# Ranking the elementwise work between two matrix products above the decoding of weights in a hand-planned attention + two-FFN kernel

## The chip, the cores and the metric

One core of one Trainium2 chip runs the whole program. The metric is the device time of one launch in microseconds; the median of three runs is compared, and one further run was profiled.

## What is computed

All numbers are float32. Attention with RMS-normalised queries and keys feeds a squared-ReLU feed-forward layer ("layer 1"), and that feeds a gated one ("layer 2"):

```python
q_n, k_n = rmsnorm(q, g_q), rmsnorm(k, g_k)               # 4 batches, 12 heads, 448 rows, 64 wide
x = softmax(q_n @ k_n.T / 8) @ v                          # -> 1792 tokens x 768
h = x @ w_in;  r = maximum(h, 0.0)                        # d_ff 2048
x = (r * r) @ w_out                                       # layer 1
g = x @ w_gate;  val = x @ w_val                          # d_ff 1536
out = (g * (1.0 / (1.0 + exp(-g))) * val) @ w_out         # layer 2
```

## The kernel before

**Three matmuls for one product.** Each float32 operand of the feed-forward layers is kept as a pair of tiles, hi and lo, whose sum is the number. A product of two 128-row blocks is three matmuls, hi with hi, hi with lo and lo with hi (`mm3`, issued at L321). One block of d_ff (128 columns, called f) against the six blocks of d_model is 18 matmuls; `in_product` makes such a group, `h`, and `out_of` adds one f to the six output tiles `y`, again 18 matmuls.

**Decoding.** The weights arrive as 64-bit words and are decoded on the chip by `load_weights`. Each of its tiles (a key such as ("in", 7)) comes as two chunks of 384 columns. A chunk is a DMA on SP's queue (`raw`), one scaling on ScalarE (L272, `wa`), four instructions on VectorE (L282, L285, L288, L291), the sum (L295, VectorE or GpSimd), the cast to hi (L212) and the difference lo (L308, VectorE or GpSimd). Slots for decoded tiles are reused: 12 from the attention phase, 8 more after it.

**The elementwise work between the two products.** In layer 1 it is `squares` for every f: ReLU on ScalarE (L356, `r`), its square on ScalarE (L357, `s` hi), the exact square on VectorE (L358, which frees the PSUM bank of `h`), and the difference (L362, `s` lo). In layer 2 it is `gated` (L373 on ScalarE, L374 on VectorE) and `valued` (L384 on VectorE, L212 on ScalarE, L387 on VectorE). There are two PSUM banks for `h` (`h_free`), three tiles for `s`, and two for `r`.

**Sweeps.** `products` runs the feed-forward layers as a list of sweeps, each one batch against a range of f. The first sweep is the last batch with f = 0 to 9, whose first three `h` are made by `lead` while attention still runs; the second is batch 2 with f = 0 to 9. `products` is one generator, so the order of the matmuls is fixed: h of f, then `out_of` for f - 2 (BEHIND = 2), then h of f + 1, and so on. The inputs of the next sweep are loaded and split by `load_x` (DMA, L212 on ScalarE, L1113 on VectorE), six tiles one after another, while the present sweep runs.

**The planner.** All of this is put in order when the program is built. `simulate` plays the kernel through with a planned cost for each operation; whenever an engine comes free it takes, among what is ready, the operation whose thread has the lowest rank, and issues it there:

```python
job = min(q, key=lambda job: (job[0].rank, job[2]))
```

What comes out is a fixed order of instructions in each engine's queue. The ranks that stand around the change: `k` is the step of a sweep that a product belongs to (POST = 10000 plus one for each f of layer 1 and two for each f of layer 2). `squares`, `gated`, `valued` and `load_x` are spawned with rank k, the writing of finished sums (`written`) with k - 2, and a weight tile that is first needed at step `when` has

```python
items += [(key, None, when[key] - W_AHEAD) for key in later]
```

with W_AHEAD = 6, and its chunk c adds c / 10. So elementwise work of step k stands behind the decoding of every tile that is due before step k + 6.

Of the kernel before, what the change touches and what calls it, by code (L numbers as in the profile page):

```python
# [52 lines left out]
W_AHEAD = 6  # L53
# [19 lines left out]
def attention_two_ffn_kernel(  # L73
# [22 lines left out]
    def as_f32(ap):  # L96
        return ap.bitcast(F32)
# [42 lines left out]
    def spawn(gen, rank, is_local=False):  # L140
        t = Thread(gen, rank, is_local)
        local[0] += is_local
        resume(t, None)
        return t

    def resume(t, value):
        while True:
            try:
                p = t.gen.send(value)
            except StopIteration:  # L150
                local[0] -= t.is_local
                return
            value = None
            serial[0] += 1
            if callable(p):
                if p():
                    continue
                blocked.append((t, p))
            elif isinstance(p, tuple):
                job = [t, p, serial[0], False]  # L160
                for e in p[0]:
                    queues["V" if e == "W" else e].append(job)
            else:
                heapq.heappush(timers, (clock[0] + p, serial[0], t, None))
            return
# [162 lines left out]
    def in_product(ps, w, x):  # L328
        for kk in range(KD):
            yield from mm3(ps, w[0], w[1], bass.ts(kk, 128), x[kk][:, 0, :], x[kk][:, 1, :], kk == 0, kk == KD - 1)  # L330
# [6 lines left out]
    def tile_at(where, shape, dtype, name):  # L337
        return where[0].tile(shape, dtype, tag=where[1], name=name)

    def h_tile(name):  # L340
        yield lambda: h_free
        where = h_free.pop(0)
        return tile_at(where, [128, S], F32, name), where

    def squares(ps, where, n, s=None):

        yield settle["P"]
        s_at = None
        if s is None:
            yield lambda: s_free  # L350
            s_at = s_free.pop(0)
            s = tile_at(s_at, [128, 2, S], F32R, f"s_{n}")
        yield lambda: ea_free
        r_at = ea_free.pop(0)
        r = tile_at(r_at, [128, S], F32, f"r_{n}")
        yield {"A": 424}, lambda e: e.activation(out=r, in_=ps, func=ACTF.Relu)  # L356
        yield {"A": 467}, lambda e: e.activation(out=s[:, 0, :], in_=r, func=ACTF.Square)  # L357
        yield {"V": 535}, lambda e: e.scalar_tensor_tensor(  # L358
            out=r, in0=ps, scalar=0.0, in1=r, op0=ALU.max, op1=ALU.mult
        )  # L360
        (h_free if where[0] is ps_f else s_banks).append(where)
        yield {"W": 535, "G": 1106}, lambda e: e.tensor_tensor(  # L362
            out=s[:, 1, :], in0=r, in1=as_f32(s[:, 0, :]), op=ALU.subtract
        )
        ea_free.append(r_at)
        ready[n] = s, s_at
# [347 lines left out]
    def all_scores(me):  # L714
        for n in range(NT):
# [9 lines left out]
            def products(e):  # L725
# [6 lines left out]
                for p, (h, rows) in enumerate(parts):  # L732
                    for c in range(2):
# [3 lines left out]
                        )  # L737

            yield {"P": 760 if full else 406 * len(parts)}, products, 0
            scored[0] = n + 1  # L740
            for h, _ in parts:
# [128 lines left out]
    def all_values(me):  # L870


        for g in range(NH // 2):
            me[0].rank = PT * g + PT - 1 + T_LAG
            slabs = range(PT * g, PT * g + PT)
            yield lambda: all(n in turned_p for n in slabs) and g in vs and o_banks
            ps = [turned_p.pop(n) for n in slabs]
            vz, vz_at = vs.pop(g)
            o_at = o_banks.pop(0)
            o = tile_at(o_at, [128, S], F32, f"o{g}")  # L880
            steps = [(h, j) for j in (3, 0, 1, 2) for h, j in ((0, j), (1, j + 4 * (j < 3)))]

            def products(e):
                for i, (h, j) in enumerate(steps):
                    half = slice(64 * h, 64 * h + 64)
                    e.matmul(o[half], lhsT=vz[:, j, half], rhs=ps[j][0], start=(i < 2), stop=(i >= 6))  # L886

            yield {"P": 3500}, products, 0
            p_free.extend(at for _, at in ps)
            v_free.append(vz_at)  # L890
            spawn(outputs(g, o, o_at), PT * g + PT - 1 + T_LAG, True)
# [206 lines left out]
    def x_tiles(n, second, ts):  # L1098
        def tile_of(j):
            pool = xp2 if second and j < 4 else xp  # L1100
            ts.append(pool.tile([128, 2, S], F32R, tag=f"x{j + 2 if second and j >= 4 else j}", name=f"x_{n}_{j}"))
            return ts[j]

        return tile_of

    def load_x(src, n, tiles, done):

        def part(j, where):
            raw = tile_at(where, [128, S], F32, f"xr_{n}_{j}")
            yield from dma(lambda e: e.dma_start(out=raw, in_=src[j]), 128 * S * 4)  # L1110
            t = tiles(j)
            yield {"A": 467, "W": 300}, lambda e: copy(e, t[:, 0, :], raw)
            yield {"W": 535, "G": 1106}, lambda e: e.tensor_tensor(  # L1113
                out=t[:, 1, :], in0=raw, in1=as_f32(t[:, 0, :]), op=ALU.subtract
            )
            io_free.append(where)
            done.append(j)

        for j in range(KD):
            yield lambda: io_free  # L1120
            yield from part(j, io_free.pop(0))

    def release(key):
        del wt[key]
        free.append(placed.pop(key))
# [3 lines left out]
    def products():  # L1129
        behind = []  # L1130
        ys = {}
        xs = x1[LAST]
        k = POST
        for i, (layer, b, fs, last_use, partial, dst) in enumerate(sweeps):
            n = f"{layer}_{i}"
            done = None
            for f in fs:
                if f == fs[X_AT if len(fs) > 6 else 1] and i + 1 < len(sweeps):
                    nxt, done = [], []
                    src = (x1_d if sweeps[i + 1][0] == 1 else x2_d)[sweeps[i + 1][1]]  # L1140
                    spawn(load_x(src, n, x_tiles(n, i % 2 == 0, nxt), done), k)
                name = f"{n}_{f}"
                if i == 0 and f < 3:
                    pass
                elif layer == 1:
                    yield lambda: ("in", f) in wt
                    ps, where = yield from h_tile(f"h_{name}")
                    yield from in_product(ps, wt["in", f], xs)
                    spawn(squares(ps, where, name), k)
                    if f in last_use:  # L1150
                        release(("in", f))
                else:
                    sig = {"n": name}
                    for w, then in (("g", gated), ("v", valued)):
                        yield lambda: (w, f) in wt
                        ps, where = yield from h_tile(f"h_{w}_{name}")
                        yield from in_product(ps, wt[w, f], xs)
                        spawn(then(ps, where, sig), k)
                        if f in last_use:
                            release((w, f))  # L1160
                while len(behind) >= BEHIND:
                    yield from behind.pop(0)
                sums = Partial(partial, n) if partial and f == fs[-1] else None
                behind.append(out_of(name, n, layer, f, f == fs[0], f == fs[-1], f in last_use, ys, sums, dst, k))
                k += layer
            if done is not None:
                yield lambda: len(done) == KD
            xs = nxt
        for gen in behind:
            yield from gen  # L1170
        finished.append(0)
# [31 lines left out]
    def out_of(name, n, layer, f, first, last, release_it, ys, sums, dst, k):  # L1203
        key = ("out" if layer == 1 else "o2", f)
        yield lambda: key in wt and name in ready
        w = wt[key]
        s, where = ready.pop(name)
        for j in range(KD):
            if first:
                ys[j] = ps_y.tile([128, S], F32, tag=f"y{j}", name=f"y_{n}_{j}")  # L1210
            yield from mm3(ys[j], w[0], w[1], bass.ts(j, 128), s[:, 0, :], s[:, 1, :], first, last)
            if last:
                spawn(written(ys[j], sums, j, n, dst[j]), k - 2)
        s_free.append(where)
        if release_it:
            release(key)

    spawn(products(), 0)
    simulate(lambda: finished and not timers and not any(queues.values()))

# [80 lines left out]
```

## Time and profile before

| | us |
|---|---|
| median of three runs | 1360.04 |
| lowest, highest | 1357.88, 1381.38 |
| the profiled execution | 1357.86 |
| its span, first to last instruction | 1356.1 |
| TensorE busy in the span | 1298.6 |
| VectorE busy | 807.2 |
| ScalarE busy | 588.3 |

Attention with the first inner products lies from 0 to about 440 us, layer 1 from there to about 819 us, and layer 2 from there to the end. Busy time is the time in which an engine had an instruction in execution; what ended an idle time is inferred from semaphores. The mean granted clock of TensorE over the span was 0.982 of full speed.

### The profile page before, as it was taken

What the parts mean: (1) busy time and instruction counts of PE and PEld (TensorE: products, weight loads), DVE (VectorE), ACT (ScalarE), POOL (GpSimd) and SP (SyncE); (2) the same over time, 40 slices, a digit from 0 to 9 for tenths busy, and PEclk for the clock granted to TensorE, in tenths of its full rate; (3) what the DMA queues carried; (4) which work ended last, traced back from release to release, by engine and by line L of the source; (5) the groups of instructions that cost most, each with busy time, mean ns of one, the idle gap of its engine ahead of it and who ended that gap; (6) DMA issues with size and microseconds to landing.
All of it is one profiled execution on the core that took longest, in us unless ns stands there. A gap on an engine that the chain in (4) does not pass through costs nothing.

```text
span 1356.1 us, 18618 instructions
## 1 busy us (share of the span) xinstructions
PE 1298.6 (96%) x6522; PEld 1111.6 (82%) x6522; DVE 807.2 (60%) x1863; ACT 588.3 (43%) x1338; POOL 185.3 (14%) x178
## 2 busy tenths in 40 slices
PE   8788899999999889999999999999999999999998
PEld 5444576666778779999999999999999999999998
DVE  7899997866641957967932299622218971213122
ACT  5787888777762524443422244321204431201100
POOL 3444434543330000000000010000000000000000
PEclk8888999999999989999999999999999999999999
DMA  6676666666511424464540356320104530303021
GB/s 198 202 227 203 202 211 215 206 207 192 177 45 67 145 94 123 146 199 127 164 149 29 109 168 210 120 82 1 61 1 141 162 102 1 109 0 116 1 82 42
DMA packets 86241, 170.75 MB, mean 126 GB/s; under 512 B 12857, under 2 KB 59778, under 8 KB 86146
## 3 DMA queue, kind: packets, MB, share of 16 engines
q1 hardware_dynamic: 86146, 169.56, 39.6%
q8 instruction: 51, 0.84, 0.3%
q14 instruction: 44, 0.36, 0.1%
HBM read 141.82 MB, written 27.69 MB: 125 GB/s over the span
## 4 chain that ended last, share of the span: by engine, by line
PE 81%; DVE 8%; DMA 6%; ACT 2%; issue 1%; POOL 1%; SPq 0%; DVEq 0%; ACTq 0%; POOLq 0%
PE y L321 26%; PE h_v L321 13%; PE h_g L321 13%; PE h L321 13%; PE o L886 4%; PE sc L734 3%; PE ya L321 2%; PE h_a L321 2%; DMA rkb<-rkd 2%; PE pt L833 2%; DMA zb<-zd 1%; DVE sc L756 1%; ACT ring L765 1%; PE pt L831 1%; POOL kst L653 1%
## 5 line engine op out<-in xcount | busy, mean ns | idle before, releaser
L321 PE MATMUL y<-s,hi_out 128*128 128x448 f32 x624 | 178.6, 367 | 4.9 <-DVE s L362 4.9
L321 PE MATMUL h<-x,hi_in 128*128 128x448 f32 x588 | 169.1, 369 | 7.5 <-DVE r L358 7.5
L321 PE MATMUL h_v<-x,hi_v 128*128 128x448 f32 x576 | 163.5, 365 | 0.0
L321 PE MATMUL h_g<-x,hi_g 128*128 128x448 f32 x576 | 163.5, 365 | 0.0
L321 PE MATMUL y<-s,hi_o 128*128 128x448 f32 x576 | 163.5, 365 | 0.0
L374 DVE TENSOR_TENSOR sig<-h_g,sig 128x448 f32<-128x448 f32 x48 | 29.9, 623 | 191.3 <-ACT sig L373 191.3
L765 ACT ACTIVATE ring<-sc,m,rms 128x448 f32<-128x448 f32 x168 | 121.8, 726 | 32.2 <-DVE m L759 22.4
L756 DVE TENSOR_REDUCE sc<-sc 128x1 f32<-128x448 f32 x168 | 101.8, 625 | 48.1 <-PE sc L734 43.5
L321 PEld LDWEIGHTS y<-s,hi_out 128*128 128x128 f32 x624 | 118.1, 189 | 14.7 <-DVE s L362 5.3
L321 PEld LDWEIGHTS h<-x,hi_in 128*128 128x128 f32 x588 | 111.8, 190 | 17.1 <-DVE r L358 8.2
L734 PE MATMUL sc<-kst,qst 128*128 128x448 f32 x368 | 108.3, 400 | 16.2 <-ACT ring L765 12.8
L321 PEld LDWEIGHTS h_g<-x,hi_g 128*128 128x128 f32 x576 | 108.2, 188 | 8.5
L321 PEld LDWEIGHTS y<-s,hi_o 128*128 128x128 f32 x576 | 108.2, 188 | 8.5
L321 PEld LDWEIGHTS h_v<-x,hi_v 128*128 128x128 f32 x576 | 108.2, 188 | 8.5
L321 PE MATMUL y<-s,lo_out 128*128 128x448 f32 x312 | 114.6, 367 | 0.0
L373 ACT ACTIVATE sig<-h_g 128x448 f32<-128x448 f32 x48 | 26.0, 542 | 191.4 <-PE h_g L321 191.4
L321 PE MATMUL h<-x,lo_in 128*128 128x448 f32 x294 | 108.4, 369 | 0.0
L321 PE MATMUL h_g<-x,lo_g 128*128 128x448 f32 x288 | 105.2, 365 | 0.0
L321 PE MATMUL y<-s,lo_o 128*128 128x448 f32 x288 | 105.2, 365 | 0.0
L321 PE MATMUL h_v<-x,lo_v 128*128 128x448 f32 x288 | 105.2, 365 | 0.0
L212 ACT COPY p<-pt 128x448 f32<-128x448 f32 x166 | 86.3, 531 | 27.7 <-PE pt L833 19.7
L734 PEld LDWEIGHTS sc<-kst,qst 128*128 128x128 f32 x368 | 62.2, 193 | 29.9 <-ACT ring L765 17.1
(160 smaller groups left out, 2335.6 us busy)
## 6 DMA issues: line engine op xcount, KB each, us to landing
kq<-in_kq_t_dram SPq DMA_DIRECT2D x46, 448.0 KB
raw_in<-in_w_in_dram SPq DMA_DIRECT2D x32, 384.0 KB
raw_out<-in_w_out_dram SPq DMA_DIRECT2D x32, 384.0 KB
vz<-in_v_z_dram SPq DMA_DIRECT2D x23, 448.0 KB
rkb<-rkd SPq DMA_DIRECT2D x46, 224.0 KB
xr<-x2d SPq DMA_DIRECT2D x42, 224.0 KB
raw_g<-in_w_gate_dram SPq DMA_DIRECT2D x24, 384.0 KB
raw_v<-in_w_val_dram SPq DMA_DIRECT2D x24, 384.0 KB
```

The source lines that it names most:

```text
L212: e.copy(out, src)
L321: return {"P": 203}, lambda e: e.matmul(ps, lhsT=w, rhs=x, start=first, stop=last), 0
L373: yield {"A": 424}, lambda e: e.activation(out=t, in_=pg, func=ACTF.Sigmoid)
L374: yield {"V": 535}, lambda e: e.tensor_tensor(out=t, in0=pg, in1=t, op=ALU.mult)
L653: yield {"G": 1106, "W": 535}, lambda e: e.tensor_tensor(out=kst[64:128], in0=kr[64:128], in1=as_f32(kst[64:128]), op=ALU.subtract)
L734: e.matmul(sc, lhsT=qs[h][:, c, rows], rhs=ks[h], start=(p + c == 0), stop=(p + 1 == len(parts) and c == 1),)
L756: yield {"V": 531}, lambda e: e.tensor_reduce(out=top, in_=sc, axis=AX.X, op=ALU.max, negate=True)
L765: yield {"A": 704}, lambda e: e.activation(out=probs(n, 0, S), in_=sc, func=ACTF.Exp, bias=m, scale=rq, accum_out=sums[g][0][:, i:i + 1])
L831: e.transpose(ps[:, at:at + 128], probs(shared, k, 128), ident)
L833: e.transpose(ps[:, bass.ts(t, 128)], probs((first if j < 3 else second) + t, k, 128), ident)
L886: e.matmul(o[half], lhsT=vz[:, j, half], rhs=ps[j][0], start=(i < 2), stop=(i >= 6))
```

## The change

Squares, gated and valued products are spawned with a rank that is W_AHEAD + 1 = 7 lower. Nothing else is edited; costs, tiles, buffers and the code of the operations stay.

```diff
@@ -1146,7 +1146,7 @@
                     yield lambda: ("in", f) in wt
                     ps, where = yield from h_tile(f"h_{name}")
                     yield from in_product(ps, wt["in", f], xs)
-                    spawn(squares(ps, where, name), k)
+                    spawn(squares(ps, where, name), k - W_AHEAD - 1)
                     if f in last_use:
                         release(("in", f))
                 else:
@@ -1155,7 +1155,7 @@
                         yield lambda: (w, f) in wt
                         ps, where = yield from h_tile(f"h_{w}_{name}")
                         yield from in_product(ps, wt[w, f], xs)
-                        spawn(then(ps, where, sig), k)
+                        spawn(then(ps, where, sig), k - W_AHEAD - 1)
                         if f in last_use:
                             release((w, f))
                 while len(behind) >= BEHIND:
```

## Rows read from the trace of the kernel before

**Rows 1.** Page: busy time; then one product in the chain (start, us, what).

```profile
PE 1298.6 (96%) x6522; PEld 1111.6 (82%) x6522; DVE 807.2 (60%) x1863; ACT 588.3 (43%) x1338; POOL 185.3 (14%) x178
...
491.09 3.65 PE h L321 x18
```

**Rows 2.** Windows: us, then busy of each engine, granted clock, DMA share, GB/s.

```profile
443.00:486.00 43.00, 30.61 (x130) 27.05 (x129) 42.88 (x104) 20.03 (x40) 0.00 (x0) 0.89 0.52 161
...
470.00:480.00 10.00, 4.71 (x17) 3.90 (x15) 9.92 (x25) 5.09 (x11) 0.00 (x0) 0.84 0.61 187
480.00:490.00 10.00, 9.13 (x32) 8.22 (x33) 7.70 (x19) 3.92 (x8) 0.00 (x0) 0.67 0.25 80
...
500.00:1356.10 856.10, 852.02 (x4205) 789.38 (x4203) 430.32 (x900) 243.91 (x479) 15.39 (x13) 1.00 0.30 97
```

**Rows 3.** Waits from 420 to 560: waiting, releaser, total us, times, longest us.

```profile
DVE r L358 <- ACT s L357: 32.1, 6, 14.8
ACT wa_out L272 <- DMA raw_out<-in_w_out_dram: 18.5, 10, 5.0
...
PE h L321 <- DVE r L358: 7.5, 2, 6.2
...
PE y L321 <- DVE s L362: 4.9, 1, 4.9
```

**Rows 4.** Timeline of TensorE: start, us, instruction, in brackets the idle before.

```profile
444.34 0.57 PE L321 MATMUL h<-x,hi_in 128*128 128x448 f32 x2
...
460.40 0.67 PE L321 MATMUL h<-x,hi_in 128*128 128x448 f32 x2 [1.31 <-DVE r L358]
...
469.44 0.61 PE L321 MATMUL y<-s,hi_out 128*128 128x448 f32 x1 [4.93 <-DVE s L362]
...
474.35 0.36 PE L321 MATMUL y<-s,lo_out 128*128 128x448 f32 x1
480.87 1.11 PE L321 MATMUL h<-x,hi_in 128*128 128x448 f32 x2 [6.16 <-DVE r L358]
...
487.28 0.57 PE L321 MATMUL y<-s,hi_out 128*128 128x448 f32 x2
```

**Rows 5.** Timeline of VectorE, 459 to 490.

```profile
459.73 0.62 DVE L358 SCALAR_TENSOR_TENSOR r<-h,r 128x448 f32<-128x448 f32 x1
460.27 0.55 DVE L308 TENSOR_TENSOR lo_out<-wt_out,hi_out 128x384 fp32r<-128x384 f32 x1
...
468.77 0.62 DVE L362 TENSOR_TENSOR s<-r,s 128x448 fp32r<-128x448 f32 x1
...
479.46 0.55 DVE L308 TENSOR_TENSOR lo_in<-wt_in,hi_in 128x384 fp32r<-128x384 f32 x1
...
480.20 0.62 DVE L358 SCALAR_TENSOR_TENSOR r<-h,r 128x448 f32<-128x448 f32 x1
...
489.21 0.61 DVE L1113 TENSOR_TENSOR x<-xr,x 128x448 fp32r<-128x448 f32 x1
```

**Rows 6.** Timeline of ScalarE in the same stretch.

```profile
458.40 0.58 ACT L357 ACTIVATE s<-r 128x448 fp32r<-128x448 f32 x1
...
473.50 0.56 ACT L272 ACTIVATE wa_out<-raw_out 128x384 f32<-128x384 f32 x1 [1.82 <-DMA raw_out<-in_w_out_dram]
...
494.08 0.56 ACT L272 ACTIVATE wa_out<-raw_out 128x384 f32<-128x384 f32 x1 [4.99 <-DMA raw_out<-in_w_out_dram]
```

**Rows 7.** Timelines later: inputs of a sweep beside their first use.

```profile
613.97 1.16 DVE L1113 TENSOR_TENSOR x<-xr,x 128x448 fp32r<-128x448 f32 x2
...
618.00 0.57 PE L321 MATMUL h<-x,hi_in 128*128 128x448 f32 x2
```

**Rows 8.** Timelines later: last gate weights of two decoding bursts beside their first use.

```profile
828.72 1.02 POOL L308 TENSOR_TENSOR lo_g<-wt_g,hi_g 128x384 fp32r<-128x384 f32 x1 [16.56 <-ACT hi_g L212]
...
873.97 0.57 PE L321 MATMUL h_g<-x,hi_g 128*128 128x448 f32 x2
...
1100.12 1.73 POOL L308 TENSOR_TENSOR lo_g<-wt_g,hi_g 128x384 fp32r<-128x384 f32 x1 [31.24 <-ACT hi_g L212]
...
1136.62 0.57 PE L321 MATMUL h_g<-x,hi_g 128*128 128x448 f32 x2
```

## The prediction

> **What bounds the kernel now.** I read the page first, then windows, then waits, then the timelines of the one stretch that was left. The page shows TensorE busy in 1298.6 of 1356.1 us [rows 1]. The change begins to act where `products` begins, at about 440 us, so only the rest counts. The windows divide that rest in two. From 500 us to the end TensorE is busy in 852.02 of 856.10 us at a granted clock of 1.00, and the missing 4 us are the last writes, behind its last matmul [rows 2]. No faster elementwise work can gain anything there: the matmuls follow each other, 3.65 us for each group of 18 [rows 1]. From 443 to 486 us the picture is another: VectorE is busy in 42.88 of 43.00 us, TensorE in only 30.61, and the granted clock falls to 0.89 [rows 2].
>
> The waits name what TensorE waits for there: twice for L358 (7.5 us together) and once for L362 (4.9 us) [rows 3]. Both are `squares`. The timeline of TensorE gives the places, three gaps of 1.31, 4.93 and 6.16 us [rows 4]. VectorE's timeline says why: for f = 4 ScalarE has finished the square at 458.98 us [rows 6], but VectorE takes its L358 up only at 480.20 us, although it is never idle for long in between [rows 2, 5]; the instructions between are decoding, such as the L308 at 460.27 [rows 5]. That is the order of the ranks. The 8 tiles of f = 6 to 9 have ranks POST to POST + 3, and the squares of f = 3, 4 and 5 have POST + 3 to POST + 5. The weights that win are not needed yet: the last chunk of ("in", 9) is done at 479.46 + 0.55 = 480.01 us [rows 5], and its product comes three h groups after the one at 480.87 [rows 4].
>
> **The change part by part.** No instruction is added or removed, and the order of matmuls is fixed by one generator. What moves is the place of `squares`, `gated` and `valued` in the queues of ScalarE, VectorE and GpSimd; they issue no DMAs. But the DMAs of raw weights on SP's queue start when L291 frees their buffer, so they move back with the decoding.
>
> *Removed, the three gaps.* After the change the squares of a step stand first on both engines once their product is done. Without gaps, TensorE runs from the h of f = 3 at 444.34 [rows 4] through seven groups (h, y, h, y, h, y and the h of f = 6) in 7 x 3.65 = 25.55 us [rows 1], to 469.89. Before, the group after them begins at 487.28 [rows 4]. The gain is 487.28 - 469.89 = 17.4 us. Taken apart: 1.31 + 4.93 + 6.16 = 12.4 us are gaps; the h from 480.87 to 487.28 takes 6.41 instead of 3.65, so 2.76 us are its slow clock (two matmuls take 1.11 instead of 0.57, the lower level of 1.2 GHz, after a gap of 6.16; the window 480 to 490 shows 0.67) [rows 2, 4]. The y from 469.44 runs 17 matmuls to 474.35 + 0.20, 5.1 instead of 17 x 3.65 / 18 = 3.45, another 1.7 us [rows 4]. The sum is 16.9; the other 0.5 us lies at the edges of the gaps. With the gaps gone the clock has no reason to fall, and I count all 17.4.
>
> *Is a square early enough?* It needs ScalarE twice and VectorE twice, 0.55 + 0.58 + 0.62 + 0.62 = 2.4 us of instructions [rows 5, 6], the ReLU taken like its neighbours. The bank is wanted again three groups after its product, 10.95 us later, and s four groups, 14.6 us later. Even a 5.0 us wait in front on ScalarE, the longest of its waits for raw weights [rows 3, 6], leaves room.
>
> *What is late next.* (a) The decoding. VectorE was full, so each square put ahead delays it. Up to 480 us five squares (f = 3 to 7) come in, ten instructions; two were there already. An L358 holds VectorE for 460.27 - 459.73 = 0.54 us [rows 5], so decoding slips by 8 x 0.54 = 4.3 us and ("in", 9) is done at 484.3. Its product, without gaps, is 12 groups after 444.34, at 488.1. Margin 3.8 us. (b) The inputs of the second sweep: their last L1113 ends at 489.8 [rows 5]. Five more square instructions ahead make it 492.5; the sixth input is wanted 14 groups and 15 matmuls after 444.34, at 444.34 + 51.1 + 3.04 = 498.5. Margin 6. (c) At the start of the fourth sweep the last split ends at 613.97 + 1.16 = 615.13 and is wanted at 618.00 [rows 7]; here the inputs lose their rank against the squares. A late square before them costs them two of 0.54 on VectorE or two on ScalarE (0.55 + 0.58), about 1.1 us for one collision and 2.3 for two. That is under 2.87, so nothing; uncovered it would cost at most 1 us. (d) Later weights: the last chunk of the sixth gate tile is there at 829.7 and wanted at 873.97, that of the twelfth at 1101.9 and wanted at 1136.62 [rows 8]. 44 and 35 us of room against a slip of a few us: nothing. (e) Finished sums now rank behind squares: four square instructions, at most 2.2 us, and an output bank is wanted again two groups (7.3 us) after its last matmul. Nothing.
>
> *Decoding pushed to GpSimd.* With squares ahead of it, L295 or L308 looks later to the planner and may go to GpSimd, where one takes 1.02 us [rows 8] instead of 0.55 on VectorE [rows 5]. In the stretch there were none [rows 2]. If VectorE loses the whole difference, three of them cost 3 x 0.47 = 1.4 us, inside margin (a); if it loses nothing they gain 3 x 0.47, inside the margin too. I take zero.
>
> The Trainium skill (SBUF — State Buffer) says that a GpSimd instruction and a VectorE instruction with two SBUF inputs cannot hold their shared port pair together, and the loser waits for the whole instruction. By that the upper figure of 1.4 us would hold, still within the margin; no row here shows such a pair.
>
> **Rivals.** *A new wait in VectorE's queue eats part of it.* An L358 at the head of VectorE's queue stands there until ScalarE's square is done, and decoding behind it stands too. For it: in this stretch VectorE waits for L357 32.1 us in all (6 times), and ScalarE itself waits for raw weights 18.5 us [rows 3]. Against it: the longest of those VectorE waits, 14.8, does not fall between 443 and 486, where it is busy all but 0.12 us [rows 2]. Priced with ScalarE's wait of 1.82 us [rows 6] before each of five squares: 9.1 us, less the margin of 3.8, is 5.3 us late at ("in", 9), and with the y's 1.7 us of slow clock after a gap of 4.93 the gain is 17.4 - 7.0 = 10.4: about 1347.5. The rival's band is 1344 to 1354.
>
> The Trainium skill (TensorE: Matmul & The Clock Gate, on the architectural detail of the array and the engines' queues) has the rule behind this: ScalarE's and VectorE's queues are strictly first in, first out. It speaks against the change, because a square placed early by the plan cannot be passed; the trace agrees, with the 32.1 us of such waits.
>
> *The ends cross: slower.* The same place with dearer waits. It decides when five waits together exceed 3.8 + 17.4 = 21.2 us, 4.2 each. With the longest raw-weight wait, 4.99 us at 494.08 [rows 6], each time: 25 us, so 21.2 late and 17.4 - 21.2 = -3.8, about 1361.7, and 1364.4 with 2.76 of slow clock. Against it: no such wait lies before 486 us in the rows I read there, where 1.82 is the longest.
>
> *It does not do what it says.* If the squares were late for their data and not for their rank, the order would stay and the time be 1357.9. Against it: the 21 us between 458.98 and 480.20.
>
> **How the numbers follow.** The profiled execution took 1357.86 us, its span 1356.1; the median of the runs, 1360.04, is 2.2 above it, the lowest, 1357.88, equal to it. 1357.86 - 17.4 = 1340.5. Chances: whole gain 0.72 (its own range 1338 to 1344, from the runs' 2.2 us and up to 3 us for (c) and GpSimd), part of it 0.16, no effect 0.05, slower 0.05, something better 0.02. From 1338 to 1352 I leave out no effect, slower and the far end of the partial case. 2% is 27 us, about what a measurement of this kernel can tell from no change; the whole gain is 1.3%. Faster by that much needs 10 us more than all the idle time on offer: 0.02. Slower by that much would need five waits of nearly 10 us: 0.02. Within 2%: 0.96.
>
> **What would show it.** Right: TensorE without a gap from 444 us on, a granted clock of 1.00 in 443 to 486, L358 within some 3 us of its L357, and ("in", 9) decoded at about 484. Wrong: a gap before the h of f = 9 at about 488 with decoding as its releaser; VectorE idle behind L357 between 443 and 486; or a gap at the start of a sweep, released by L1113.

## The result, and the profile after

The changed kernel takes 1344.43 us in the median of ten runs (1338.38 to 1354.48); the kernel before, run beside it, 1362.1 (1357.88 to 1381.38). The ratio is 0.9884 with a 95% interval of 0.9848 to 0.9921, so 1.2% less time, within the 2% that counts as the same. The ratio is of fast runs alone, so it leaves out the kernel before's run of 1381.38 us, a slow one. The prediction was 1340.5 us, 1.3% less, with a range of 1338 to 1352. The profiled execution of the changed kernel took 1339.4 us, its span 1337.6.

The stretch that [rows 2] show as 30.61 of 43.00 us of TensorE at a clock of 0.89 is full now. The windows of the changed kernel, columns as before:

```profile
443.00:486.00 43.00, 43.00 (x214) 39.84 (x214) 43.00 (x104) 21.91 (x44) 0.00 (x0) 1.00 0.51 157
470.00:480.00 10.00, 10.00 (x51) 9.27 (x50) 10.00 (x25) 5.75 (x13) 0.00 (x0) 1.00 0.43 133
...
500.00:1337.60 837.60, 832.89 (x4110) 771.67 (x4108) 426.49 (x892) 240.16 (x471) 14.61 (x13) 1.00 0.31 99
```

TensorE is busy in all of it at a granted clock of 1.00, and VectorE is still full, 43.00 against 42.88: it does the same kind of work in another order. No wait of TensorE after 440 us is left in the trace. What answers to [rows 4] is a plain row of groups. TensorE's timeline of the changed kernel, with the first h of `products` (f = 3), the h of f = 9 and the last matmul:

```profile
442.62 0.57 PE L321 MATMUL h<-x,hi_in 128*128 128x448 f32 x2
...
486.40 0.57 PE L321 MATMUL h<-x,hi_in 128*128 128x448 f32 x2
...
1332.53 0.36 PE L321 MATMUL y<-s,lo_o 128*128 128x448 f32 x1
```

From the h of f = 3 to the last matmul this is 889.91 us. Before it was 1351.65 - 444.34 = 907.31, the last matmul read from this row of the kernel before:

```profile
1351.65 0.36 PE L321 MATMUL y<-s,lo_o 128*128 128x448 f32 x1
```

The difference is 17.40 us, the number predicted. The rest of the profiled difference of 18.5 us was not foreseen as an effect of the change: the attention phase, whose instructions are the same, ended 1.72 us earlier in this execution (442.62 against 444.34), and the time behind the last matmul's start is 0.62 us longer (5.07 against 4.45).

VectorE's timeline, against [rows 5]:

```profile
458.31 0.61 DVE L358 SCALAR_TENSOR_TENSOR r<-h,r 128x448 f32<-128x448 f32 x1
...
459.11 0.61 DVE L362 TENSOR_TENSOR s<-r,s 128x448 fp32r<-128x448 f32 x1
...
481.81 0.54 DVE L308 TENSOR_TENSOR lo_in<-wt_in,hi_in 128x384 fp32r<-128x384 f32 x1
...
486.23 0.61 DVE L1113 TENSOR_TENSOR x<-xr,x 128x448 fp32r<-128x448 f32 x1
```

The first two rows are f = 4. ScalarE's square of it, in ScalarE's timeline, is

```profile
457.27 0.58 ACT L357 ACTIVATE s<-r 128x448 fp32r<-128x448 f32 x1
```

and VectorE takes L358 up 0.46 us after its end, where it came 21 us after [rows 5, 6]. The third row is the last chunk of ("in", 9), the price: done at 482.35 us, 2.3 us later than before although the h of f = 3 began 1.7 us earlier, still 4 us ahead of its own h at 486.40. The fourth is the last input of the second sweep.

The waits from 420 to 560 us, against [rows 3]; columns as there:

```profile
DVE r L358 <- ACT s L357: 16.4, 2, 14.8
...
ACT wa_out L272 <- DMA raw_out<-in_w_out_dram: 12.8, 11, 1.8
ACT wa_in L272 <- DMA raw_in<-in_w_in_dram: 12.0, 11, 2.7
```

No line names TensorE any more. VectorE's wait of 14.8 us is the old one ahead of 443 us.

### The profile page after: what moved, and what is told of

Its sections match the earlier page's. It is cut to its first block, busy times and chain, and to the rows that moved or that the text cites. A ratio compares the mean times of both kernels' runs of the same rounds, so it can differ in the third digit from the quotient of the medians.

```text
span 1337.6 us, 18609 instructions
## 1 busy us (share of the span) xinstructions
PE 1292.4 (97%) x6522; PEld 1108.8 (83%) x6522; DVE 808.0 (60%) x1863; ACT 589.4 (44%) x1338; POOL 186.3 (14%) x178
## 4 chain that ended last, share of the span: by engine, by line
PE 81%; DVE 8%; DMA 4%; ACT 3%; issue 2%; SPq 1%; POOL 1%; DVEq 0%; ACTq 0%; POOLq 0%
PE y L321 27%; PE h L321 13%; PE h_v L321 13%; PE h_g L321 13%; PE sc L734 3%; PE o L886 3%; PE ya L321 2%; DVE sc L756 2%; PE h_a L321 2%; PE pt L833 1%; ACT ring L765 1%; DMA zb<-zd 1%; DMA rkb<-rkd 1%; PE pt L831 1%; PE h_lead L321 1%
## 6 DMA issues: line engine op xcount, KB each, us to landing
kq<-in_kq_t_dram SPq DMA_DIRECT2D x46, 448.0 KB
vz<-in_v_z_dram SPq DMA_DIRECT2D x23, 448.0 KB
```

## The experiments

The measure that the runs share is the stretch from the first matmul of the h of f = 3 to the end of the span, because attention ahead of it varies (that h began between 442.2 and 448.0 us in the profiles) and the change does not act there. It is 911.8 us in the kernel before and 895.0 in the changed one.

**Where the gain lies: the first sweep alone, and all but the first.**

```diff
-spawn(squares(ps, where, name), k - W_AHEAD - 1)
+spawn(squares(ps, where, name), k - (W_AHEAD + 1) * (i == 0))   # gated, valued: k
```

> Squares get the new rank in the first sweep alone (f = 3 to 9 of the last batch); all later squares, gated and valued products keep rank k. Theory (the whole gain is the three gaps between 459 and 481 us and the slow clock after them): TensorE without a gap from the h of f = 3 on, the stretch from that h to the end as short as with the whole change, 895.0 us in the changed kernel's trace (442.62 to 1337.6), and a time about 17 us under the kernel before. Rival (later sweeps contribute): the stretch is some us longer than 895 and gaps or a slow clock are left after 500 us.

Measured: 1340.99 us in the median of six runs; ratio to the kernel before, as it ran in that job, 0.9795 (0.9749 to 0.9842). The stretch is 1336.9 - 442.58 = 894.3 us, without a gap.

```diff
-spawn(squares(ps, where, name), k - W_AHEAD - 1)
+spawn(squares(ps, where, name), k - (W_AHEAD + 1) * (i > 0))    # gated, valued: k - W_AHEAD - 1
```

> The complement: the new rank everywhere but in the first sweep. Theory: the three gaps (1.3, 4.9 and 6.2 us, released by L358 and L362) are back and the time is that of the kernel before, within 2 us in the stretch from the h of f = 3 to the end (911.8 us in its trace, 444.34 to 1356.1). Rival (later sweeps contribute): the stretch is clearly under 911.8.

Measured: 1360.46 us in the median of twelve; ratio 0.9941 (0.9902 to 0.9979). The stretch is 1355.3 - 443.48 = 911.8 us, and TensorE's timeline has the three gaps back:

```profile
459.52 0.68 PE L321 MATMUL h<-x,hi_in 128*128 128x448 f32 x2 [1.28 <-DVE r L358]
468.56 0.74 PE L321 MATMUL y<-s,hi_out 128*128 128x448 f32 x1 [4.85 <-DVE s L362]
479.92 0.74 PE L321 MATMUL h<-x,hi_in 128*128 128x448 f32 x1 [4.97 <-DVE r L358]
```

So the seven squares of f = 3 to 9 in one sweep are the whole effect; every other spawn that the diff touches gains nothing. (These ratios stand against 17 runs of the kernel before with a median of 1373.15 us, one of them of 3170.85 us whose cause is not known; that is why they lie lower than the result's. The stretches do not have that trouble; the last section says what may lie behind the 1373.)

**The same from the other side: decoding ranked lower.** The kernel before, with one constant changed:

```diff
-W_AHEAD = 6
+W_AHEAD = 2
```

> The kernel before with W_AHEAD = 2 instead of 6 and the ranks of squares untouched: the weights of f = 6 to 9 get ranks POST + 4 to POST + 7, behind the squares of f = 3 to 6. Theory (only the order of the two in VectorE's queue counts, not that squares stand first of all): the three gaps go from this side too, and the stretch from the h of f = 3 to the end is 895 to 898 us. Rival (decoding that ranks lower everywhere comes too late somewhere): new gaps released by L308 or L212, and less of the 17 us.

Measured: 1341.46 us in the median of four, ratio 0.9796 (0.9742 to 0.9851); the stretch is 1339.8 - 445.39 = 894.4 us, no gap. The gain does not need squares that stand above everything; it needs an order in which the weights of f = 9 do not stand ahead of the squares of f = 4 and, as the run with `k - 1` below shows, of f = 5.

**How much of the rank is needed.** `k - 3` and `k - 1` in place of `k - W_AHEAD - 1`.

> The changed kernel with rank k - 3 instead of k - 7. The square of f then ties with the weights of f + 3, and precedes all later ones. Theory (a square need only pass the weights that are not wanted soon): the square of f = 4 waits for decoding up to f = 6 or 7 at most, its bank is free well before 466 us, and no gap is left: 895 us from the h of f = 3 to the end. Rival (only rank above everything is enough): at least one of the three gaps remains.

Measured: the stretch is 1341.2 - 446.19 = 895.0 us, no gap.

> The changed kernel with rank k - 1. The squares of f = 3, 4 and 5 rank with the weights of f = 8, 9 and behind them. Theory: L362 of f = 3 and L358 of f = 4 still wait for most of the decoding but not for its last tiles; gaps before the y of f = 3 and the h of f = 6 stay but are shorter; 899 to 908 us from the h of f = 3 to the end. Rival (any step of rank frees them): 895 us; or the gaps are as before: 911.8 us.

Measured: 1365.7 - 443.43 = 922.3 us, outside the 899 to 908 expected, with one gap (a pause of 0.2 us before the h of f = 5 aside), and that one in a place that was not expected:

```profile
480.84 0.74 PE L321 MATMUL h<-x,hi_in 128*128 128x448 f32 x1 [7.73 <-DVE r L358]
```

This is the h of f = 7, not that of f = 6. VectorE's timeline shows what it waited for: the L358 of f = 5, whose rank POST + 4 is the first one behind the last chunk of ("in", 9), POST + 3.1, and it came right behind that chunk's L308:

```profile
479.44 0.54 DVE L308 TENSOR_TENSOR lo_in<-wt_in,hi_in 128x384 fp32r<-128x384 f32 x1
479.91 0.34 DVE L288 TENSOR_SCALAR wa_out<-wt_out 128x384 int32<-128x384 int32 x1
480.18 0.61 DVE L358 SCALAR_TENSOR_TENSOR r<-h,r 128x448 f32<-128x448 f32 x1
```

One step of rank lets f = 3 and f = 4 through in time and leaves f = 5 where f = 4 was. The expectation had put f = 3 and f = 4 behind the tiles that they tie with. The gap and the slow clock behind it do not explain 27 us more than 895; the last section comes back to that.

**How much room the decoding has left.** The changed kernel with the last subtraction of each square of f = 3 to 9 repeated on VectorE, the same values written again.

```diff
+        for _ in range(2 if n[:4] == "1_0_" and int(n[4:]) > 2 else 0):     # 4 in the second run
+            yield {"W": 535}, lambda e: e.tensor_tensor(
+                out=s[:, 1, :], in0=r, in1=as_f32(s[:, 0, :]), op=ALU.subtract
+            )
```

> The changed kernel with the last subtraction of each square in the first sweep (f = 3 to 9) written two more times on VectorE, 1.07 us more for each square. It measures margin (a) of the prediction. Five squares stand ahead of the last chunk of (in, 9): 5 x 2 x 0.535 = 5.4 us later, so 482.35 + 5.4 = 487.7 against the h of f = 9 at 486.4, whose second half, which reads that chunk, begins at 488.2. Theory: no gap or one of at most 1.3 us, and the rest as in the changed kernel (895 to 897 us from the h of f = 3 to the end). Rival (VectorE's queue has no such reserve, squares at its head block it): gaps of several us from 458 us on.

Measured: one gap, before the second half of the h of f = 9 (it began at 491.80 us, its tenth matmul at 495.35):

```profile
495.35 0.66 PE L321 MATMUL h<-x,hi_in 128*128 128x448 f32 x2 [1.57 <-ACT hi_in L212]
```

That is the place and, against at most 1.3, nearly the size. But the stretch is 913.1 us, 18 more than the 895 to 897 expected, and no second gap is there.

> As the run with two more, but four more subtractions for each square of the first sweep, 2.14 us more each. Theory: (in, 9) is done at about 482.35 + 10.7 = 493 us or somewhat later, 5 to 8 us behind the second half of its h at 488.2; one gap of that size there, released by decoding, followed by a slow clock for some us; the stretch from the h of f = 3 to the end is 901 to 907 us, so part of the gain is lost. Rival (decoding has far more reserve, since the plan moves some of it to GpSimd): no gap, 895 us.

Measured: five gaps of 0.38, 0.58, 5.72, 1.17 and 0.47 us, all for ("in", 8) and ("in", 9), at the second halves of the h of f = 8 and of f = 9 and, the largest, at the start of the h of f = 9:

```profile
496.98 1.11 PE L321 MATMUL h<-x,hi_in 128*128 128x448 f32 x2 [5.72 <-ACT hi_in L212]
```

The largest has the size that was expected, the sum of 8.3 us is a little above it, and decoding is the releaser in both runs: what comes next, when squares cost more, is margin (a). The stretch, 922.5 us, is again 15 us or more beyond the 901 to 907 expected.

> The run with two more subtractions per square once more, unedited. Its stretch from the h of f = 3 to the end was 913.1 us, of which its one gap of 1.57 us explains little; 18 matmuls took 3.71 us instead of 3.65 after that gap. Theory (that pace is a draw at the gap, not a cost of the edit): the gap is there again at the second half of the h of f = 9, and the stretch is either about 897 us or again about 913. Rival (the edit itself slows the matmuls): 913 and a slow pace from before the gap.

Measured: 913.1 us again, the gap again at the same matmul, 1.58 us. The matmuls are slow only behind the gap, so the repeated subtractions, most of which lie ahead of it, do not slow them. The same outcome twice does not tell a draw at the gap from an outcome that is fixed by what went before it.

**The changed kernel again.**

> The changed kernel once more, unedited. Its ten times lie between 1338 and 1354 us. Theory: the stretch from the h of f = 3 to the end is either 895 us, or, at the slower pace of 3.71 us for 18 matmuls, 895 x 3.71 / 3.65 = 910 us, and the stretch before it varies by a few us; no gap after 440 us either way. Rival: the times differ by gaps or by the granted clock after 440 us.

> The same once more, for the same question: 895 us or about 910 us from the h of f = 3 to the end, without a gap.

Measured: 1339.64 and 1342.84 us; stretches 1337.9 - 442.91 = 895.0 and 1341.1 - 446.00 = 895.1 us, without a gap. Of the 3.2 us between them 3.1 lie ahead of the h of f = 3.

**The pace of matmuls by itself.** Two kernels in which nothing of the reference is computed: series of 90 matmuls and, between them, copies on ScalarE for which the next series waits.

```diff
+    for i in range(SERIES):                       # 56 series, then 48
+        ps = pp.tile([128, S], F32, tag=f"ps{i % 2}", name=f"h{i}")      # i % 3 in the second
+        ... 5 groups of 18 matmuls, hi hi lo ...
+        nc.scalar.copy(t, ps)
+        for _ in range(PAUSE[i % len(PAUSE)]):    # 0, 4, 9, 16; then 0, 2, 7, 14, 1
+            nc.scalar.copy(t, xr[:, 1, :])        # in the second into x, so that the series waits
+        for c in range(2):
+            nc.scalar.copy(x[:, c, :], xr[:, c, :])
```

> The disputed cost by itself: nothing of the reference is computed. 56 series of 90 matmuls of 128x448 in the order hi hi lo of the kernel, and between the series a chain on ScalarE of 3, 7, 12 or 19 copies (0.5 to 0.6 us each) for which TensorE waits. In the runs with extra work and with rank k - 1 a group of 18 matmuls took 3.65 us before a pause with a slow clock and 3.71 after it, to the end, at a granted clock of 1.00 both times. Theory (the pace is drawn anew when the clock comes back, whatever the kernel): after the longer pauses the settled spacing of matmuls takes one of two values, about 203 and 206 ns, and changes from series to series; after pauses too short for the clock to fall it keeps the value that it had. Rival (it is the kernel's memory traffic or its instruction order): one spacing in all series.

Measured: the pauses all came out near 1.35 us, since the extra copies ran beside the matmuls. Yet from the third series on the settled spacing alternates strictly, 206.7 ns in one series and 202.4 to 202.9 in the next, at a granted clock of 1.00. The theory was wrong in two things: the clock need not fall for the pace to change, and a strict alternation (54 of the 55 pauses changed the pace) is not a draw.

> Nothing of the reference is computed. As the run of series alone, where the pauses all came out at 1.35 us and the spacing alternated strictly between 206.7 and 202.6 ns, even and odd series, which is also the change of PSUM bank. Now three banks in turn instead of two, and pauses that go round five lengths (0, 2, 7, 14 and 1 more copies, about 0.5 us each, in front of the next series). Theory (the spacing is drawn at each pause): it no longer follows the series' parity; both values occur in each bank and after pauses of each length, also those without a fall of the granted clock. Rival (it goes by the bank): one bank of three has always the same value.

Measured, settled spacing worked out from the starts in the last 7 us of each series:

| pause before the series, us | series near 202.6 ns | series at 206.7 ns |
|---|---|---|
| 1.35 | 1 | 9 |
| 1.94 | 9 | 0 |
| 2.6 | 1 | 9 |
| 5.5 | 2 | 7 |
| 9.7 | 4 | 5 |

The pauses of 1.35 and of 1.94 us fall on all three banks in turn, so the bank is not it. Length alone is not it either, and its rows are not independent, because each length always follows the same one. In the run of series alone a pause of 1.35 us led from fast to slow and from slow to fast in turn; here every series before such a pause was fast, and nine of ten went slow. After 2.6 us the pace stayed what it had been in all ten series, nine times slow and once fast; after 1.94 us it was fast each time, whatever it had been. So the theory that it is drawn anew at each pause does not hold as it stands: the pace before a pause counts, and the pause's length does.

## Why the prediction was right

*What bounds the kernel.* Right, and tested from both sides: the stretch from 443 to 486 us alone holds the gain, and after 500 us the matmuls keep their pace and have no gap in either kernel.

*The size.* 17.4 us were forecast as three gaps, slow clock behind two of them and edges; 17.40 us were measured to the last matmul. The mechanism and its size are shown; that the two agree to 0.01 us is also luck. Both profiled executions ran at 3.65 us for 18 matmuls after the last gap, and the last section shows that a gap can end at a pace of 3.72 instead, which is worth some 16 us and which the prediction did not have. The end added 0.62 us that no step had: 5.06 to 5.10 us behind the start of the last matmul in the result, both repeats, all but the first sweep, k - 3 and k - 1, against 4.41 to 4.50 in the kernel before, the first sweep alone and W_AHEAD = 2. But the three runs with added subtractions, which have the change in the later sweeps too, show 4.44 to 4.49, so it does not go with the change alone. Why is open.

*Is a square early enough?* Yes. The product of f = 4 ended with its group at 453.56 us, and its L362 at 459.11 + 0.61 = 459.72: 6.2 us, not the 2.4 of the instructions alone, but its bank was free at 458.92, and the h of f = 6 that wants it began at 464.51.

*What is late next.* (a) ("in", 9) was forecast at 484.3 us on the old time axis; 1.72 us earlier is 482.6, and it came at 482.35. The margin of 3.8 us was too small, because the last chunk is read only from the tenth matmul of its group on: the run with two more subtractions stalls there and not at the group's start. 1.8 us belong to it, 5.6 in all, and 5.4 us of added subtractions led to a gap of 1.57. Decoding slipped more than they count: the chunk was done 495.89 - 448.02 = 47.9 us after the first h instead of 482.35 - 442.62 = 39.7, so 8.1 us later; the 2.7 us beyond the 5.4 are not explained. (b) The last input of the second sweep was forecast at 492.5, which is 490.8 on the new axis, and came at 486.84. Its split on VectorE had been held before by ScalarE's queue, where a ReLU waited for a late product; that wait went with the gaps. (c) The last split of the fourth sweep's inputs and the matmul that wants it, against [rows 7]:

```profile
594.85 1.15 DVE L1113 TENSOR_TENSOR x<-xr,x 128x448 fp32r<-128x448 f32 x2
...
598.88 0.57 PE L321 MATMUL h<-x,hi_in 128*128 128x448 f32 x2
```

It was done at 596.00, 2.88 us ahead where it was 2.87 before: no collision came. (d) and (e): no gap of any releaser after 440 us.

*The rivals.* A wait of VectorE behind ScalarE did not arise: between 443 and 486 us VectorE was busy in 43.00 of 43.00 us. The rule of strictly first-in-first-out queues in the Trainium skill (TensorE: Matmul & The Clock Gate, on the engines' queues) was not contradicted: an L358 waited for its L357 twice between 420 and 560 us, 16.4 us together, of which the 14.8 lie ahead of 443 us. In the stretch no square at the head of the queue was late. That this is because TensorE no longer ran late against the plan is likely and was not tested. The slower end falls with it, and the order of the queue did change.

*The time.* The median, 1344.4, is 4 us above the 1340.5, which was counted from the profiled execution of the kernel before (1357.86) and not from its median. In the three profiles of the changed kernel the stretch is 894.98, 894.99 and 895.10 us and its start 442.62, 442.91 and 446.00, so what varies there lies in attention. The longest of the ten times, 1354.48, is beyond what these starts explain.

## What to carry to other kernels

When a planner ranks work by due times, ask of every wait of the bounding engine what stood ahead of its releaser and when that was needed: here a square that freed a bank TensorE was already waiting for stood behind weights done at 480.01 us [rows 5], whose h in the kernel before began 25 us later:

```profile
505.52 0.57 PE L321 MATMUL h<-x,hi_in 128*128 128x448 f32 x2
```

Putting the bulk work later (W_AHEAD = 2) or the short work earlier (by 3) gives the same 17 us; the question to check is the reserve of what is pushed back, and the first place where it ends. When what lies ahead of a change varies by as much as a good part of the gain, compare versions by the stretch from a fixed instruction to the end and not by the whole time, and look at the pace of the matmuls in that stretch as well.

## What the runs showed of the hardware that was not expected

TensorE has two paces at a granted clock of 1.00, and a short wait can change from one to the other for the rest of a run. In the run with two more subtractions the windows ahead of the gap of 1.57 us and behind it, columns as in [rows 2], are

```profile
450.00:490.00 40.00, 40.00 (x200) 37.12 (x199) 39.90 (x91) 18.53 (x36) 5.47 (x1) 1.00 0.45 137
510.00:550.00 40.00, 40.00 (x196) 36.34 (x195) 38.74 (x89) 22.69 (x48) 0.00 (x0) 1.00 0.61 188
900.00:940.00 40.00, 40.00 (x196) 36.34 (x195) 8.56 (x15) 8.45 (x17) 0.00 (x0) 1.00 0.21 69
```

and its chain of waits has groups of 3.72 us instead of the 3.65 of [rows 1]:

```profile
508.82 3.72 PE h L321 x18
```

From the end of that h to the last matmul the changed kernel takes 1332.53 - 490.05 = 842.5 us and this run 1356.61 - 497.50 = 859.1. These 16.6 us and the 1.57 of the gap are the 18 that were missing. The same pace stands from the gap to the end in the run with four more subtractions and in the one with k - 1 (195 or 196 matmuls in 40 us, where the kernel before and the changed one have 199 or 200). It is no property of the chip that a run fell on: k - 3 kept 3.65 on the same chip as k - 1, and so did the first sweep alone on that of the run with two more. In the kernel of series alone with varied pauses it is the bare matmul. Two series, the first after a pause of 1.94 and the second after one of 1.35 us:

```profile
141.04 0.36 PE L116 MATMUL h<-x,w 128*128 128x448 f32 x1
...
144.08 0.36 PE L116 MATMUL h<-x,w 128*128 128x448 f32 x1
...
148.33 0.37 PE L117 MATMUL h<-x,w 128*128 128x448 f32 x1
...
150.81 0.37 PE L117 MATMUL h<-x,w 128*128 128x448 f32 x1
```

Fifteen matmuls in 3.04 us, 202.7 ns each, and twelve in 2.48, 206.7. The last gap of the kernel before, 6.16 us, happened to end at the faster pace, and so did that of the run with all but the first sweep, 4.97; those of the run with two more subtractions (1.57 and 1.58), of k - 1 (7.73) and of the run with four more ended at the slower one. What selects the pace was not settled. It may also make part of the scatter of whole runs. The kernel before ran, beside the result and beside the first three variants, either in 1357.55 to 1364.31 us or in 1370.41 to 1381.38 (the one of 3170.85 aside), with nothing between, and the distance is near those 16 us. But no profile of the kernel before or of the changed one shows the slower pace, so this is not shown.

With VectorE full and more work ahead of it, the plan moved the splitting of inputs (L1117 in those kernels' numbering) to GpSimd, not decoding: one with two more subtractions, three with four more. The first took 5.47 us in the one run and 6.07 in the other, beside 1.25 and 1.59 for the later two, though GpSimd's spans are rough. GpSimd's timeline of the run with four more:

```profile
456.52 6.07 POOL L1117 TENSOR_TENSOR x<-xr,x 128x448 fp32r<-128x448 f32 x1 [30.11 <-ACT x L212]
465.12 1.25 POOL L1117 TENSOR_TENSOR x<-xr,x 128x448 fp32r<-128x448 f32 x1 [2.52 <-ACT x L212]
471.83 1.59 POOL L1117 TENSOR_TENSOR x<-xr,x 128x448 fp32r<-128x448 f32 x1 [5.45 <-ACT x L212]
```

VectorE's timeline in the same run has the counterpart of the two later ones. The repeated subtraction (L366 there), 0.61 us elsewhere, and L282, 0.35 us elsewhere, end 0.5 and 0.2 us after GpSimd's instruction:

```profile
465.28 1.57 DVE L366 TENSOR_TENSOR s<-r,s 128x448 fp32r<-128x448 f32 x1
...
472.33 1.31 DVE L282 TENSOR_SCALAR wt_out<-wa_out 128x384 int32<-128x384 int32 x1
```

That agrees with the rule of the Trainium skill (SBUF — State Buffer, on the two separate sides of SBUF) that the loser of the shared port pair waits for the other's whole instruction, with VectorE as the loser here; that the wait is the port's was not tested. One such wait of GpSimd, behind a VectorE instruction of 0.6 us, would not make the 5.47 and 6.07 us of its first. In both runs that first one ended 1.1 us after an L358 had begun (461.50 and 463.09 us), which reads one of its inputs from PSUM; whether GpSimd had lost to a dozen instructions in a row until then is open.
